# Column cuts of the second MoE product: 512-column products parted, first pairs at 280 and 232, last pairs at 304 and 208

## Chip, cores and metric

The kernel runs on one core of a Trainium2 chip. Times are device microseconds of one execution; the time before is the median of three runs, 930.46 us (929.8 to 931.54). The profile is of one further execution of the same kernel, which took 930.22 us.

## What is computed

Chunked attention over 8 batches, 8 heads, 576 positions, in chunks of 64, then a mixture-of-experts layer with a rational activation, all in float32:

```python
scores = scale * np.matmul(q_c, k_c.transpose(0, 1, 2, 4, 3))
scores = scores - np.max(scores, axis=-1, keepdims=True)
attn = np.exp(scores)
attn = attn / (np.sum(attn, axis=-1, keepdims=True) + 1e-09)
out = np.matmul(attn, v_c)
...
h = x @ w_in                      # 4608 x 512 @ 512 x 2048
h2 = h * h
h3 = h2 * h
P = a[0] + a[1] * h + a[2] * h2 + a[3] * h3
Q = 1.0 + np.abs(b[0]) * np.abs(h) + np.abs(b[1]) * h2
g = P / (Q + 1e-06)
return (g @ w_out).astype(np.float32)   # 4608 x 2048 @ 2048 x 512
```

## The kernel before

The 4608 tokens are cut into 18 groups of 256 (`NB`, index n). Of each group the 2048 hidden columns are cut into four stages of 512 (`NST`, index s). A step g is one pair (n, s). Matmul operands are kept as two parts, a rounded one and the rest (wi_hi and wi_lo, wo_hi and wo_lo, xhi and xlo, ghi and glo), and each product is made of three of them.

FF1 (`ff1`, L329) of a step is 48 products: for each of four blocks of 128 hidden columns, four blocks of 128 rows of x, three combinations. The weights part is stationary (128 columns), x is moving (256 columns, the tokens). It writes the PSUM tile ph.

The rational function of ph is worked out on ScalarE and VectorE (`chain_a` to `chain_glo`) and gives ghi and glo.

FF2 (`ff2`, L393) is the other way round: g is stationary (128 tokens), wo is moving (512 output columns). Parts 0 and 1 are the 16 combinations of ghi with wo_hi and wo_lo, part 2 the 8 of glo with wo_hi. Each of the 24 combinations is run as two products of 256 columns with the same stationary operand, columns 0 to 255 and 256 to 511, so a step has 48. Exceptions are the four products of a group that open or close a PSUM bank: these are single ones of 512 columns. FF2 accumulates all four stages of a group in the tile po, two banks (i = 0 and 1 for the two halves of the tokens). The line that picks the cuts:

```python
for c in ([slice(0, DM)] if start or stop else [slice(0, 256), slice(256, DM)]):
```

with `start` in stage 0 at the first wo_hi product of each bank (k of 0 and 2 of part 0), and `stop` in stage 3 at the last glo product of each bank (k of 3 and 7 of part 2). In the built program each product comes with a load of its stationary operand (LDWEIGHTS), also where two in a row have the same.

Attention of the next group runs between: scores and values (`quarters`, L203: 64 small products of 64 x 64 each; tiles pss and psx), and eight transposes (L282, tile pst).

The program is in an order written by hand (`manual_schedule`). Up to step 11 it is the string `START`, in which a letter stands for an operation and a number for a step or group (F, f: FF1; Z, z, y: the three parts of FF2; S scores; T transposes; A values). From step 12 on the loop at L464 writes it: in each step FF1 of step g, then the attention work of the next group that belongs to the stage, then FF2 of step g - 2 (`LAG`). In TensorE's order one group is:

| stage of g | TensorE runs |
|---|---|
| 0 | FF1, scores, FF2 of the previous group's stage 2 |
| 1 | FF1, FF2 of the previous group's stage 3 (two 512-column products at its end), transposes |
| 2 | FF1, values, FF2 of this group's stage 0 (two 512-column products at its start) |
| 3 | FF1, FF2 of this group's stage 1 |

Of the kernel before, what the change touches and what calls it, by code (L numbers as in the profile page):

```python
# [23 lines left out]
DM = 512  # L24
DFF = 2048
FPS = 4
NST = DFF // (128 * FPS)
# [18 lines left out]
)  # L46
FIRST = 12
PL_TAG = {0: "po", 1: "p1"}

PIECES = [(m, fq, k) for m, fq in ((0, 0), (0, 1), (1, 0), (0, 2), (1, 1), (0, 3), (1, 2), (1, 3)) for k in (0, 1)]  # L50
# [3 lines left out]
def tile_chunked_attention_rational_moe(  # L54
# [32 lines left out]
    def bank_pair(tag, name):  # L87
        return ps.tile([P, 2, 512], F32, tag=tag, name=name)
# [56 lines left out]
    def words(j):  # L145
        low, high = raws[j][:, :, 0], raws[j][:, :, 1]
        return low, high, high.bitcast(F32)

    def w_dest(j):
        return place(j, (wi_hi, wo_hi), (wi_lo, wo_lo))  # L150
# [26 lines left out]
    def w_rest(j):  # L177
        val, hi = words(j)[2], w_dest(j)[0]
        pls[j] = bank_pair(PL_TAG.get(j, "pa"), f"pl{j}")
        n = hi.shape[1] // 2  # L180
# [13 lines left out]
    def groups_of(u):  # L194
        return slice(0, NQ) if u is None else slice(u * NHP, (u + 1) * NHP)

    def quarters(out_cols, tile_out, stat, mov, u):
        for g in range(NQ)[groups_of(u)]:
            for par in range(2):
                for c in range(2):  # L200
                    rows = slice(64 * c, 64 * c + 64)
                    cols = slice(g * 128 + par * 64, g * 128 + par * 64 + 64)
                    nc.tensor.matmul(  # L203
                        tile_out[par * 64:(par + 1) * 64, c, out_cols(g)],
                        stat[rows, cols], mov[rows, cols], start=True, stop=True,
                    )
# [12 lines left out]
    def att_s(n, u=None, tag="pa"):  # L219
        pss = have("s", n, lambda: bank_pair(tag, f"pss{n}"))  # L220
        quarters(lambda g: slice(g * 64, g * 64 + 64), pss, loaded["q", n], loaded["k", n], u)
# [68 lines left out]
    def att_av(n, u=None, tag="pa"):  # L290
        psx = have("x", n, lambda: bank_pair(tag, f"psx{n}"))

        def cols(g):
            v, hp = divmod(g, NHP)
            return slice(hp * 128 + v * 64, hp * 128 + v * 64 + 64)

        quarters(cols, psx, loaded["v", n], att["at", n], u)
# [18 lines left out]
    ch, gbuf, obuf = {}, {}, {}  # L316

    def ff1(n, s, tag, part):
        xhi, xlo = xbuf[n]
        if part == 0:  # L320
            ch[n, s] = [bank_pair(tag, f"ph{n}_{s}").rearrange("p a (b t) -> p (a b) t", t=BT), None, None, None]
        ph = ch[n, s][0]
        for fi in range(2 * part, 2 * part + 2):
            f = slice((FPS * s + fi) * P, (FPS * s + fi + 1) * P)
            mm = []
            for cc in range(NHP):
                mm += [(wi_hi, xhi, cc), (wi_hi, xlo, cc), (wi_lo, xhi, cc)]
            for k, (w, x, cc) in enumerate(mm):
                nc.tensor.matmul(ph[:, fi, :], w[:, cc, f], x[:, cc, :], start=(k == 0), stop=(k == len(mm) - 1))  # L329
# [48 lines left out]
        nc.vector.tensor_mul(gbuf[n, s][1], B, A)  # L378


    def ff2(n, s, tag, part):
        if s == 0 and part == 0:
            obuf[n] = bank_pair(tag, f"po{n}")
        ghi, glo = gbuf[n, s]
        if part < 2:
            mm = [(ghi, w, fi, i) for fi in (2 * part, 2 * part + 1) for i in range(2) for w in (wo_hi, wo_lo)]
        else:
            mm = [(glo, wo_hi, fi, i) for i in range(2) for fi in range(FPS)]
        for k, (g, w, fi, i) in enumerate(mm):
            start = s == 0 and part == 0 and k in (0, 2)  # L390
            stop = s == NST - 1 and part == 2 and k in (3, 7)
            for c in ([slice(0, DM)] if start or stop else [slice(0, 256), slice(256, DM)]):
                nc.tensor.matmul(  # L393
                    obuf[n][:, i, c], g[:, fi, i * 128:(i + 1) * 128], w[:, FPS * s + fi, c], start=start, stop=stop,
                )

    def store(n, last=False):

        rows = out[n * BT:(n + 1) * BT, :].rearrange("(u c t) f -> c u t f", u=UPB, c=2)
        o = p2.tile([P, 2, DM], F32, tag="eo", name=f"o{n}")  # L400
        po = obuf.pop(n)
        if last:
            nc.scalar.copy(o[:, 0, :], po[:, 0, :])
            nc.vector.tensor_copy(o[:, 1, :], po[:, 1, :])
        else:
            nc.scalar.copy(o, po)
        for c in range(2):
            for u in range(UPB):
                nc.sync.dma_start(out=rows[c, u], in_=o[64 * u:64 * u + 64, c, :])

    steps = [(n, s) for s in range(NST) for n in (0, 1)] + [(n, s) for n in range(2, NB) for s in range(NST)]
# [34 lines left out]
    for k, letter in enumerate("Ff"):  # L446
        do[letter] = lambda g, k=k: ff1(*steps[g], ph_tag(g), k)
    for k, letter in enumerate("Zzy"):
        do[letter] = lambda g, k=k: ff2(*steps[g], po_tag(steps[g][0]), k)
# [13 lines left out]
    total = len(steps)  # L463
    for g in range(FIRST, total + LAG):  # L464
        n, s = steps[min(g, total - 1)]
# [59 lines left out]
```

## Time and profile before

| | before |
|---|---|
| median of 3 runs | 930.46 us |
| profiled execution | 930.22 us |
| its span, first to last instruction | 928.4 us |
| TensorE matmul busy | 886.0 us (95%), 9306 products |
| TensorE weight loads busy | 867.7 us (93%), 9306 loads |
| VectorE busy | 746.9 us (80%) |
| ScalarE busy | 593.9 us (64%) |
| DMA | 55.87 MB, mean 60 GB/s |

TensorE's matmuls are pipelined: the profile's duration of one (some 280 ns for 256 columns) overlaps the next, so the pace of a run of products is read from start to start, or from the length of a run divided by its products. In the view of the chain each row has the start of a piece in microseconds after the span's start, its length, the engine, the tile written, the line and the number of instructions; consecutive instructions of one line are merged.

### The profile page before, as it was taken

Reading aid. Unit: us, or ns where it says so; the run is one execution under the profiler, and the core shown is the slowest. Engines: PE = TensorE matmul, PEld = TensorE weight load, DVE = VectorE, ACT = ScalarE, POOL = GpSimd, SP = SyncE. Lnnn points to the kernel's source line nnn. Section 1 sums busy time; section 2 is a strip of 40 time slices with the busy share of each in tenths; the row PEclk is TensorE's granted clock in tenths of the full one; section 3 lists DMA queues with packets and bytes.
Section 4 is the critical chain, followed back from the end, with each engine's and each line's share of the span. In section 5 each row is a group of like instructions: output and inputs, shape, how many; then the busy total and the mean of one; then the engine's idle time right before and its main releaser. Section 6 shows DMA issues by size and latency. Waiting matters only on the chain.

```text
span 928.4 us, 20908 instructions
## 1 busy us (share of the span) xinstructions
PE 886.0 (95%) x9306; PEld 867.7 (93%) x9306; DVE 746.9 (80%) x668; ACT 593.9 (64%) x984; POOL 0.8 (0%) x8
## 2 busy tenths in 40 slices
PE   3589899999999999999999999999999999999997
PEld 2578899999999999999999999999999999999997
DVE  5788888798787878787878787878787888878774
ACT  5999688757474747475757575656565656565452
POOL 0000000000000000000000000000000000000000
PEclk9779899999999999999999999999999999999999
DMA  8443531202020202011110202020202020101011
GB/s 295 165 152 137 181 117 44 55 16 92 1 92 1 86 7 63 30 38 55 24 70 10 83 1 92 2 92 1 92 2 92 2 92 2 47 1 24 1 24 23
DMA packets 20601, 55.87 MB, mean 60 GB/s; under 512 B 2592, under 2 KB 2592, under 8 KB 20512
## 3 DMA queue, kind: packets, MB, share of 16 engines
q1 hardware_dynamic: 20512, 54.54, 18.1%
q8 instruction: 73, 1.20, 0.5%
q14 instruction: 16, 0.13, 0.0%
HBM read 45.09 MB, written 9.44 MB: 59 GB/s over the span
## 4 chain that ended last, share of the span: by engine, by line
PE 82%; ACT 12%; DVE 3%; DMA 2%; issue 1%; SPq 0%; ACTq 0%
PE po L393 39%; PE ph L329 38%; ACT raw L162 3%; PE psx L203 2%; DMA raw<-in_w_in 2%; PE pss L203 2%; ACT raw L158 1%; PE pst L282 1%; ACT e L258 1%; ACT wo_hi L169 1%; ACT A L334 1%; ACT A L349 1%; ACT C L341 1%; ACT B L337 1%; ACT A L353 1%
## 5 line engine op out<-in xcount | busy, mean ns | idle before, releaser
L329 PE MATMUL ph<-xhi,wi_hi 128*128 128x256 f32 x1152 | 326.2, 283 | 8.6 <-DVE C L361 5.2
L329 PE MATMUL ph<-xlo,wi_hi 128*128 128x256 f32 x1152 | 324.2, 281 | 1.6 <-DVE xlo L313 1.6
L329 PE MATMUL ph<-xhi,wi_lo 128*128 128x256 f32 x1152 | 323.6, 281 | 0.0
L334 ACT ACTIVATE A<-ph,ab 128x1024 f32<-128x1024 f32 x72 | 81.3, 1129 | 273.7 <-PE ph L329 272.0
L393 PE MATMUL po<-wo_hi,ghi 128*128 128x256 f32 (+1 forms) x1116 | 230.6, 285 | 3.2 <-DVE ghi L366 3.2
L329 PEld LDWEIGHTS ph<-xhi,wi_hi 128*128 128x128 f32 x1152 | 221.5, 192 | 10.1 <-issue 4.1
L393 PE MATMUL po<-wo_lo,ghi 128*128 128x256 f32 x1152 | 227.5, 279 | 0.0
L329 PEld LDWEIGHTS ph<-xlo,wi_hi 128*128 128x128 f32 x1152 | 219.3, 190 | 2.3 <-DVE xlo L313 2.2
L329 PEld LDWEIGHTS ph<-xhi,wi_lo 128*128 128x128 f32 x1152 | 219.5, 191 | 0.0
L345 DVE SCALAR_TENSOR_TENSOR B<-B,ab,A 128x1024 f32<-128x1024 f32 x72 | 92.4, 1284 | 112.9 <-ACT B L337 112.9
L393 PEld LDWEIGHTS po<-wo_lo,ghi 128*128 128x128 f32 x1152 | 177.9, 188 | 1.6
L393 PEld LDWEIGHTS po<-wo_hi,ghi 128*128 128x128 f32 x1116 | 171.1, 188 | 5.7 <-DVE ghi L366 3.4
L393 PE MATMUL po<-wo_hi,glo 128*128 128x256 f32 (+1 forms) x1116 | 146.9, 284 | 1.9 <-DVE glo L378 1.9
L393 PEld LDWEIGHTS po<-wo_hi,glo 128*128 128x128 f32 x1116 | 137.2, 189 | 3.2 <-DVE glo L378 2.4
L366 DVE SCALAR_TENSOR_TENSOR ghi<-C,ab,A 128x1024 fp32r<-128x1024 f32 x72 | 92.4, 1284 | 11.0 <-ACT A L353 2.4
L349 ACT ACTIVATE A<-B,cst 128x1024 f32<-128x1024 f32 x72 | 83.9, 1166 | 26.4 <-DVE B L345 26.3
L361 DVE SCALAR_TENSOR_TENSOR C<-C,ab,ph 128x1024 f32<-128x1024 f32 x72 | 92.2, 1280 | 3.2 <-ACT B L337 1.0
L374 DVE SCALAR_TENSOR_TENSOR B<-C,ab,B 128x1024 f32<-128x1024 f32 x72 | 92.5, 1285 | 2.4
L378 DVE TENSOR_TENSOR glo<-B,A 128x1024 fp32r<-128x1024 f32 x72 | 88.2, 1225 | 6.8
L357 DVE TENSOR_TENSOR C<-C,ph 128x1024 f32<-128x1024 f32 x72 | 87.5, 1215 | 4.5 <-ACT B L337 3.6
L370 DVE SCALAR_TENSOR_TENSOR B<-B,ghi 128x1024 f32<-128x1024 f32 x72 | 88.2, 1225 | 2.3
L341 ACT ACTIVATE C<-ph,ab 128x1024 f32<-128x1024 f32 x72 | 88.0, 1222 | 2.5 <-DVE B L374 2.3
(53 smaller groups left out, 712.4 us busy)
## 6 DMA issues: line engine op xcount, KB each, us to landing
v<-in_vP SPq DMA_DIRECT2D x18, 512.0 KB, 4.0
out<-o SPq DMA_DIRECT2D x72, 128.0 KB, 2.4
raw<-in_w_in SPq DMA_DIRECT2D x8, 1024.0 KB, 6.6
raw<-in_w_out SPq DMA_DIRECT2D x8, 1024.0 KB, 5.9
qk<-in_qT SPq DMA_DIRECT2D x16, 512.0 KB, 4.7
qk<-in_kT SPq DMA_DIRECT2D x16, 512.0 KB, 5.7
Aqk<-in_qT SPq DMA_DIRECT2D x2, 256.0 KB, 3.4
Bqk<-in_kT SPq DMA_DIRECT2D x2, 256.0 KB, 4.0
```

The costliest lines, as they stand in the source:

```text
L329: nc.tensor.matmul(ph[:, fi, :], w[:, cc, f], x[:, cc, :], start=(k == 0), stop=(k == len(mm) - 1))
L334: nc.scalar.activation(ch[n, s][1], ch[n, s][0], AF.Abs, scale=b0)
L341: nc.scalar.activation(ch[n, s][3], ch[n, s][0], AF.Identity, bias=a2, scale=a3)
L345: nc.vector.scalar_tensor_tensor(B, B, b1a, A, ALU.mult, ALU.add)
L349: nc.scalar.activation(A, B, AF.Ln, bias=cst[:, 0:1], scale=2.0 ** -KLN)
L357: nc.vector.tensor_mul(C, C, h)
L361: nc.vector.scalar_tensor_tensor(C, C, a1, h, ALU.add, ALU.mult)
L366: nc.vector.scalar_tensor_tensor(gbuf[n, s][0], C, a0, A, ALU.add, ALU.mult)
L370: nc.vector.scalar_tensor_tensor(B, B, CQ, gbuf[n, s][0].bitcast(F32), ALU.add, ALU.mult)
L374: nc.vector.scalar_tensor_tensor(B, C, a0, B, ALU.add, ALU.subtract)
L378: nc.vector.tensor_mul(gbuf[n, s][1], B, A)
L393: nc.tensor.matmul(obuf[n][:, i, c], g[:, fi, i * 128:(i + 1) * 128], w[:, FPS * s + fi, c], start=start, stop=stop,)
```

## The change

No product of FF2 has 512 columns any more: each combination is run as two. The cut between the two is column 256, with two exceptions. The first pair of a step's FF2 is cut at 280 (280 and 232 columns) where the matmuls issued last before it were `quarters`, that is scores or values. The last pair of a step's FF2 is cut at 304 (304 and 208 columns), except in the last three steps of the kernel. A small record, `before`, holds which of the three functions issued matmuls last while the program is written. The flag `start` is on the first product of a bank alone, `stop` on the last alone.

```diff
+CUT_FIRST, CUT_LAST = 24, 48
...
+    before = [""]
+
     def quarters(out_cols, tile_out, stat, mov, u):
+        before[0] = "quarters"
...
     def ff1(n, s, tag, part):
         xhi, xlo = xbuf[n]
+        before[0] = "ff1"
...
         for k, (g, w, fi, i) in enumerate(mm):
-            start = s == 0 and part == 0 and k in (0, 2)
-            stop = s == NST - 1 and part == 2 and k in (3, 7)
-            for c in ([slice(0, DM)] if start or stop else [slice(0, 256), slice(256, DM)]):
+            cut = 256
+            if part == 0 and k == 0 and before[0] == "quarters":
+                cut += CUT_FIRST
+            if part == 2 and k == len(mm) - 1 and (n, s) not in steps[-3:]:
+                cut += CUT_LAST
+            for c in (0, 1):
+                start = s == 0 and part == 0 and k in (0, 2) and c == 0
+                stop = s == NST - 1 and part == 2 and k in (3, 7) and c == 1
+                cols = slice(cut, DM) if c else slice(0, cut)
                 nc.tensor.matmul(
-                    obuf[n][:, i, c], g[:, fi, i * 128:(i + 1) * 128], w[:, FPS * s + fi, c], start=start, stop=stop,
+                    obuf[n][:, i, cols], g[:, fi, i * 128:(i + 1) * 128], w[:, FPS * s + fi, cols], start=start, stop=stop,
                 )
+        before[0] = "ff2"
```

TensorE's program, in the loop, behind values (psx7 are the values of group 7, po6 and ghi6_0 the FF2 of group 6, stage 0; the last number of a name is a buffer's). Before:

```order
L203 MATMUL psx7_3994<-at7_3936,v7_3459 64x64 x32
L393 MATMUL po6_4043<-wo_hi_69,ghi6_0_3752 128x512
L393 MATMUL po6_4043<-wo_lo_70,ghi6_0_3752 128x256 x2
L393 MATMUL po6_4043<-wo_hi_69,ghi6_0_3752 128x512
L393 MATMUL po6_4043<-wo_lo_70,ghi6_0_3752 128x256 x2
L393 MATMUL po6_4043<-wo_hi_69,ghi6_0_3752 128x256 x2
```

and now:

```order
L207 MATMUL psx7_4018<-at7_3960,v7_3479 64x64 x32
L405 MATMUL po6_4067<-wo_hi_69,ghi6_0_3774 128x280
L405 MATMUL po6_4067<-wo_hi_69,ghi6_0_3774 128x232
L405 MATMUL po6_4067<-wo_lo_70,ghi6_0_3774 128x256 x2
L405 MATMUL po6_4067<-wo_hi_69,ghi6_0_3774 128x256 x2
L405 MATMUL po6_4067<-wo_lo_70,ghi6_0_3774 128x256 x2
```

The two 512-column products have become pairs, the first of them uneven. Behind scores (FF2 of stage 2) the first pair is uneven in the same way, and no 512-column product stood there.

TensorE's program at the end of FF2 of group 6, stage 3, ahead of the transposes of group 8 (pst8) and FF1 of group 7, stage 2 (ph7_2). Before:

```order
L393 MATMUL po6_4043<-wo_lo_70,ghi6_3_4150 128x256 x2
L393 MATMUL po6_4043<-wo_hi_69,glo6_3_4151 128x256 x6
L393 MATMUL po6_4043<-wo_hi_69,glo6_3_4151 128x512
L393 MATMUL po6_4043<-wo_hi_69,glo6_3_4151 128x256 x6
L393 MATMUL po6_4043<-wo_hi_69,glo6_3_4151 128x512
L282 MATMUL pst8_4495<-ident_71,e8_4303 128x128 x8
L329 MATMUL ph7_2_4506<-xhi7_4033,wi_hi_67 128x256
```

and now:

```order
L405 MATMUL po6_4067<-wo_lo_70,ghi6_3_4176 128x256 x2
L405 MATMUL po6_4067<-wo_hi_69,glo6_3_4177 128x256 x14
L405 MATMUL po6_4067<-wo_hi_69,glo6_3_4177 128x304
L405 MATMUL po6_4067<-wo_hi_69,glo6_3_4177 128x208
L286 MATMUL pst8_4523<-ident_71,e8_4329 128x128 x8
L334 MATMUL ph7_2_4534<-xhi7_4057,wi_hi_67 128x256
```

Here too both 512-column products are gone, and the last pair is uneven. At the ends of the other FF2 runs, where FF1 follows directly, the last two of 16 products with glo have become one of 304 and one of 208 columns; nothing else stands differently there. Over the whole program TensorE has 72 products more, 29 first pairs and 69 last pairs are uneven, and the programs of the other engines are unchanged.

## The prediction

> **What bounds the kernel now.** First the page: busy shares, the granted TensorE clock by slices, and the shares of the chain that ended last.
>
> ```profile
> PE 886.0 (95%) x9306; PEld 867.7 (93%) x9306; DVE 746.9 (80%) x668; ACT 593.9 (64%) x984; POOL 0.8 (0%) x8
> PEclk9779899999999999999999999999999999999999
> PE 82%; ACT 12%; DVE 3%; DMA 2%; issue 1%; SPq 0%; ACTq 0%
> ```
>
> TensorE is busy 95% of the span and holds 82% of the chain, at full clock after the first fifth. A busy share of pipelined matmuls doesn't say how quick they go, so the second view is the chain in order of time over one turn of the loop (start us, us, what): ph is FF1, po FF2, pss scores, psx values, pst transposes.
>
> ```profile
> 430.43 5.44 PE po L393 x48
> 435.87 5.65 PE ph L329 x48
> 441.52 1.09 PE pss L203 x64
> 442.62 5.64 PE po L393 x48
> 448.26 5.66 PE ph L329 x48
> 453.92 5.66 PE po L393 x46
> 459.58 0.87 PE pst L282 x8
> 460.45 5.46 PE ph L329 x48
> 465.91 1.09 PE psx L203 x64
> 467.00 5.85 PE po L393 x46
> 472.85 5.46 PE ph L329 x48
> 478.30 5.44 PE po L393 x48
> 483.75 5.65 PE ph L329 x48
> ```
>
> Each piece begins where the last ended: nothing but TensorE is on the path, and what it saves here the kernel saves. And the same work has **two paces**. 48 products of 256 columns take 5.44 to 5.46 us (113.3 ns each) or 5.65 to 5.66 (117.8). FF2 has it too: 5.44 directly behind a quick FF1, 5.66 behind a slow one; behind scores or values, where some 0.2 us of entry is in the piece, 5.64 or 5.85. A stretch keeps the pace with which it begins. In this turn four of the eight stretches are slow: 435.87, 448.26, 453.92 and 467.00.
>
> The third view, busy times of stretches (span; PE, PEld, DVE, ACT, POOL; clock), says that this isn't the clock, and how often the turn occurs.
>
> ```profile
> 435.71:483.58 47.87, 47.87 (x518) 47.26 (x517) 38.87 (x35) 29.24 (x56) 0.00 (x0) 1.00 0.15 46
> 244.22:866.57 622.35, 622.35 (x6711) 614.47 (x6709) 505.28 (x443) 380.19 (x716) 0.00 (x0) 1.00 0.13 41
> ```
>
> The clock is 1.00 throughout, and 622.35 / 47.87 is 13 turns. VectorE works 38.87 us of the 47.87, so a turn of 47.1 us leaves it 8 us. The chain outside these turns:
>
> ```profile
> 157.63 4.15 ACT e L258 x28
> 169.18 5.92 PE ph L329 x48
> 190.85 5.65 PE po L393 x48
> 196.50 5.45 PE ph L329 x48
> 203.05 5.85 PE po L393 x48
> 208.89 5.66 PE ph L329 x48
> 214.55 5.66 PE po L393 x46
> 227.63 5.85 PE po L393 x46
> 866.73 5.66 PE ph L329 x48
> 872.39 5.66 PE po L393 x48
> 888.97 5.46 PE ph L329 x48
> 894.43 5.64 PE po L393 x46
> 900.07 5.66 PE ph L329 x48
> 905.73 16.98 PE po L393 x142
> ```
>
> Until about 167 us the chain goes through ScalarE and VectorE (the 157.63 row is of that stretch), so a faster TensorE brings nothing there; from 169.18 on it is TensorE's.
>
> What sets a stretch's pace? The rows give four rules. FF2 directly behind FF1 inherits: 472.85 and 478.30 are both quick, 448.26 and 453.92 both slow. FF1 behind a quick FF2 is slow (430.43 then 435.87, 442.62 then 448.26); behind a slow FF2 it is mostly quick (467.00 then 472.85), but not always (894.43 then 900.07). Behind the transposes it is quick (460.45). And a 512-column product ends a quick pace: 894.43 follows the quick FF1 of 888.97 and would inherit 5.44, but begins with such a product and takes 5.64.
>
> **The change part by part.** Only PE's program differs.
>
> *The 72 products of 512 columns go* and become 144 of two parts. What one costs stands in the timeline (start us, us, instruction):
>
> ```profile
> 894.27 0.39 PE L393 MATMUL po<-wo_hi,ghi 128*128 128x512 f32 x1
> 894.49 0.40 PE L393 MATMUL po<-wo_lo,ghi 128*128 128x256 f32 x2
> 894.73 0.40 PE L393 MATMUL po<-wo_hi,ghi 128*128 128x512 f32 x1
> 894.97 0.40 PE L393 MATMUL po<-wo_lo,ghi 128*128 128x256 f32 x2
> ```
>
> The next start comes 0.22 us after the first and 0.24 after the second: as long as two halves at either pace, so parting costs between nothing and 72 x 0.01 = 0.7 us less or more; I take nothing, the 0.22 being 2 x 113 ns to the row's last digit. The added weight load lies under the first half. What it brings is that a quick FF2 stays quick through its start and stop.
>
> *The last pair at 304 and 208.* At 5.44/48 = 113.3 ns per 256 columns, 304 take 134.6 ns and 208 take 92. But the product behind the 208 needs its weights, loaded only once the 208 has begun. The nearest row is the eight transposes, 128 columns and a load each: 0.87/8 = 109 ns; the other end is the 113.3. So the pair takes 243 to 248 ns in place of 226.7: **17 to 21 ns dearer**, I take 19, midway. 69 FF2 runs have it, some 62 of them after 167 us: 62 x 19 ns = **+1.2 us** (1.0 to 1.3). The Trainium skill ("TensorE: Matmul & The Clock Gate", Back-to-back issue gap and LDWEIGHTS) has 2.5 ns + N/2.4 for a product and P/1.2 for a load; by it the pair takes 129.2 + 106.7 in place of 2 x 109.2, 17.5 ns more, and the sum would be +1.1, though it has 109 ns where this trace has 113.3 or 117.8.
>
> *The first pair at 280 and 232* comes 29 times, behind scores or values:
>
> ```profile
> 442.55 0.50 PE L393 MATMUL po<-wo_hi,ghi 128*128 128x256 f32 x2
> 442.88 0.39 PE L393 MATMUL po<-wo_lo,ghi 128*128 128x256 f32 x2
> ```
>
> The second product started 0.50 - 0.28 = 0.22 us after the first: it waits for its weights, and 280 columns (124 ns) are hidden under that. 232 columns (103 ns) are shorter than any load pace above. Cost: nothing (at most 29 x 0.01 = 0.3 if the 280 did show).
>
> *What the two pairs bring* the trace before can't show directly: neither form occurs. Both do one thing: behind the shorter part TensorE waits for the weights with nothing in flight, and the next product begins at another moment against its load. The nearest entry of that kind is that from transposes into FF1 (short products, each waiting for its load), 460.45: quick. Against it speaks the entry behind scores and values, also load-bound, which gave 5.64 at 442.62 and 5.85 at 203.05 and 467.00. So per entry the worth lies between a whole stretch turned quick and one turned slow. I take quick for all, nearest to the 460.45 row, and the rivals hold the other ends.
>
> The sum, each piece at the slow pace replaced by the quick one of the same surroundings: per turn 435.87 5.65 to 5.45 (as 196.50, also ahead of scores), 448.26 5.66 to 5.46, 453.92 5.66 to 5.44, 467.00 5.85 to 5.64: 0.83, times 13 is 10.8. From 190 to 244 us: 190.85, 203.05, 208.89, 214.55, 227.63 give 0.21 + 0.21 + 0.20 + 0.22 + 0.21 = 1.05; from 169 to 190, of 5.92 and some short pieces, 0.4 (0 to 0.7). At the end 0.20 + 0.22 + 0.20 + 0.20, and 16.98 to 144 x 0.1133 = 16.32: together 1.48. Sum 13.7 saved, 1.2 spent. The profiled execution's own time is 930.22 (span 928.4 and 1.8 around it): 917.7; the median shown is 0.24 above it, so **917.9**. Behind a faster TensorE nothing is late: VectorE has the 8 us above. If its cover were gone, TensorE would wait for ghi, and a turn would stay above 38.87.
>
> **The rivals.**
>
> *B: the last pair works, the first doesn't.* For it: FF2 at 203.05 was slow behind scores that followed a quick FF1, and now every FF1 would be quick. Then FF2 behind scores turns slow (-0.21) and FF2 behind values stays so: per turn 0.20 + 0.20 + 0.22 - 0.21 = 0.41, times 13 is 5.3; 0.6 before, 0.4, 1.5 after; less 1.2: **923.9**.
>
> *C: only the price.* The entry doesn't decide, or decides as before, and four of eight stretches stay slow: 930.46 + 1.2 = **931.7**. Against it: 894.43 shows one product's form changing a stretch's pace. The Trainium skill (same page, Step-by-step: what each phase is for) says that weights and moving operand have read ports of their own, so that a load takes nothing from a running matmul. By that one pace is to be had and C follows; the trace, with two paces of one form at clock 1.00, disagrees so far.
>
> *D, on the slower side: the last pair is a bad entry.* If the FF1 behind it begins as FF1 behind a quick FF2 does now, all such FF1 are slow and the FF2 directly behind inherits. Place: 472.85 and 478.30, now quick, 0.20 + 0.22 lost per turn, 5.5 in 13, some 1.2 outside, and the price 1.2: **938.3**. The point where it decides: four last pairs cost 4 x 19 = 76 ns a turn, so the change loses as soon as it doesn't take away at least 0.4 of a slow-paced stretch per turn, net.
>
> **How the numbers follow.** Forecast A 0.47 (its own range 916.3 to 919.6, by the price, the 0 to 0.7 and the parting), B 0.22, C 0.15, D 0.16. A measurement here tells 0.2%, 1.9 us, from no change. A and B are faster: 0.69; C, 931.7, is within 0.2%: 0.15; D is slower: 0.16. The range reaches from A's lower end over B and C, and leaves out D and some 0.04 below: 916.0 to 932.4.
>
> **What would show it.** In the chain of the changed kernel FF1 at 5.44 to 5.48 behind FF2 with its last pair shows the second step right; 5.65 shows it wrong. FF2 behind scores and values at 5.64 shows the first pair right, 5.85 wrong. FF2 behind the last FF1 of a token group at 5.44, start and stop included, shows the 512s to have been what ended the quick pace. The last pair's price stands in the timeline, as the time from the 304 to the first FF1 product. Wrong would be the forecast if pieces of ScalarE or VectorE entered the chain after 250 us, or if entries were not alike from turn to turn.

## The result and the profile after

| | before | changed |
|---|---|---|
| time, median of 4 runs each | 931.0 us (929.8 to 932.11) | 920.46 us (920.09 to 921.43) |
| profiled execution | 930.22 us, span 928.4 | 920.15 us, span 918.3 |

The ratio is 0.9889 [0.9872, 0.9906]: 1.1% faster. The median moved by 10.5 us where 12.6 were forecast.

The page of the changed kernel, busy shares and the chain that ended last:

```profile
PE 874.2 (95%) x9378; PEld 859.6 (94%) x9378; DVE 747.0 (81%) x668; ACT 593.4 (65%) x984; POOL 0.8 (0%) x8
PE 82%; ACT 11%; DVE 2%; DMA 2%; issue 1%; SPq 1%; ACTq 0%
```

TensorE runs 72 products more than before and is busy 11.8 us less (886.0 to 874.2); the busy times of the other engines and the shares of the chain are the same to within 0.5 us and a point. The time has gone out of TensorE's own pace. One turn of the loop, by the chain in order of time (start us, us, what):

```profile
433.46 5.48 PE ph L334 x48
438.94 1.09 PE pss L207 x64
440.03 5.66 PE po L405 x48
445.69 5.48 PE ph L334 x48
451.17 5.45 PE po L405 x48
456.62 0.87 PE pst L286 x8
457.49 5.46 PE ph L334 x48
462.95 1.09 PE psx L207 x64
464.04 5.66 PE po L405 x48
469.70 5.48 PE ph L334 x48
475.19 5.44 PE po L405 x48
480.63 5.48 PE ph L334 x48
```

All eight stretches (a stretch is one FF1 or FF2 of 48 products) have the quick pace, 5.44 to 5.48, or 5.66 with the entry behind scores or values in it. Before, four were slow. The turn is 480.63 - 433.46 = **47.17 us**; it was 483.75 - 435.87 = 47.88.

The start and the end of the part that TensorE bounds, from the same view (the row of 244.76 is cut off where that view ended):

```profile
169.81 5.92 PE ph L334 x48
...
191.56 5.66 PE po L405 x48
197.22 5.66 PE ph L334 x48
202.88 1.09 PE pss L207 x64
203.97 5.85 PE po L405 x48
209.82 5.49 PE ph L334 x48
...
244.76 5.25 PE ph L334 x46
```

```profile
858.02 5.48 PE ph L334 x48
...
896.28 16.34 PE po L405 x144
```

With the rows of before these split the whole gain. The FF1 that opens the first turn starts at 244.76 in place of 244.38: 0.38 us later. Thirteen turns from there (to 858.02, as 866.73 before) take 613.26 in place of 622.35: 9.09 less. From there to the end of the last FF2 it is 912.62 - 858.02 = 54.60 in place of 55.98: 1.38 less. Together 10.1, the difference of the spans.

### The profile page after: what moved, and what is told of

Read it like the earlier page. It is cut to its first block, busy times and chain, and to the rows that moved or that the text cites. A ratio compares the mean times of both kernels' runs of the same rounds, so it can differ in the third digit from the quotient of the medians.

```text
span 918.3 us, 21052 instructions
## 1 busy us (share of the span) xinstructions
PE 874.2 (95%) x9378; PEld 859.6 (94%) x9378; DVE 747.0 (81%) x668; ACT 593.4 (65%) x984; POOL 0.8 (0%) x8
## 4 chain that ended last, share of the span: by engine, by line
PE 82%; ACT 11%; DVE 2%; DMA 2%; issue 1%; SPq 1%; ACTq 0%
PE po L405 39%; PE ph L334 38%; ACT raw L163 3%; PE psx L207 2%; PE pss L207 2%; DMA raw<-in_w_in 2%; ACT raw L159 2%; PE pst L286 1%; ACT e L262 1%; ACT A L339 1%; ACT wo_hi L170 1%; ACT A L354 1%; ACT B L342 1%; ACT C L346 1%; ACT A L358 1%
## 5 line engine op out<-in xcount | busy, mean ns | idle before, releaser
L334 PE MATMUL ph<-xhi,wi_hi 128*128 128x256 f32 x1152 | 325.2, 282 | 10.1 <-DVE C L366 6.7
L405 PE MATMUL po<-wo_hi,ghi 128*128 128x256 f32 (+2 forms) x1152 | 228.9, 280 | 3.2 <-DVE ghi L371 3.2
L405 PEld LDWEIGHTS po<-wo_hi,ghi 128*128 128x128 f32 x1152 | 174.1, 188 | 5.7 <-DVE ghi L371 3.4
L405 PEld LDWEIGHTS po<-wo_lo,ghi 128*128 128x128 f32 x1152 | 174.4, 189 | 0.0
L405 PE MATMUL po<-wo_hi,glo 128*128 128x256 f32 (+2 forms) x1152 | 143.3, 277 | 1.6 <-DVE glo L383 1.6
```

What stands on the lines that cost most here:

```text
L405: nc.tensor.matmul(obuf[n][:, i, cols], g[:, fi, i * 128:(i + 1) * 128], w[:, FPS * s + fi, cols], start=start, stop=stop,)
```

## The experiments

Each kernel ran once, with a run of the kernel before on the same chip beside it. Single times scatter: the chain reaches TensorE's part anywhere from 168.33 to 171.93 us in these runs, ahead of the stretches that are compared here. So the verdicts go by the length of a turn, 47.88 before and 47.17 after, which repeats thirteen times in one run, and by which of its eight stretches are slow. In the view of each kernel's loop the turn repeats to 0.01 us (in p7 below it alternates between two values). The place where one stretch ends and the next begins is called a seam. In the tables the stretches are named by place: A is FF1 ahead of the scores, B FF2 behind them, C and D the next FF1 and FF2, E FF1 behind the transposes, F FF2 behind the values, G and H the next FF1 and FF2. All edits are made to the changed kernel; CUT_FIRST and CUT_LAST are what is added to 256 columns in the first part of the first and of the last pair.

### The parts of the change one by one

```diff
-CUT_FIRST, CUT_LAST = 24, 48
+CUT_FIRST, CUT_LAST = 0, 0     e1_parted_only
+CUT_FIRST, CUT_LAST = 0, 48    e2_last_only
+CUT_FIRST, CUT_LAST = 24, 0    e3_first_only
```

> All pairs cut at 256, no 512-column product. Entry theory (the way a stretch's first product meets its weight load sets the stretch's pace, and the uneven pairs change that): the turn stays at 47.87 us as before, four of eight stretches at 5.65, about 930 us. Rival, the 512-column products alone ended the quick pace: the turn falls to 47.1, about 918 us.

> Only the last pair uneven (304 and 208), first pair at 256. Entry theory: FF1 stays at 5.48 behind FF2, FF2 behind scores and behind values goes from 5.66 to 5.85, the turn from 47.17 to 47.55, about 926 us. Rival, the first pair isn't needed once no product has 512 columns: the turn stays at 47.15.

> Only the first pair uneven (280 and 232), last pair at 256. Entry theory: FF2 behind scores and values stays at 5.66, but each FF1 behind a quick FF2 begins slow and the FF2 directly behind inherits: five stretches slow, the turn about 48.0 us, longer than before, about 934 us. Rival, each uneven pair is worth its own stretches: FF2 behind values gains 0.2 and nothing is lost, the turn 47.65, about 927 us.

| kernel | time us | before, beside it | turn us | slow stretches |
|---|---|---|---|---|
| before | | 930.68 | 47.88 | A, C, D, F |
| e1: 512s parted, all pairs even | 934.66 | 930.68 | 48.28 | B, C, D, F, G, H |
| e2: and the last pair 304 and 208 | 933.42 | 930.68 | 48.14 | B, C, D, E, F |
| e3: and the first pair 280 and 232 | 930.73 | 930.68 | 47.90 | C, D, G, H |
| changed: both | 920.15 | | 47.17 | none |

The turn follows the number of slow stretches, at 0.18 to 0.2 us each. But the parts don't add up. Against the run of before beside them, parting alone costs 4.0 us, parting with the last pair 2.7, parting with the first pair 0.0, and all three together bring 10.1. So neither the expectation nor the rival of e1 and of e2 came out, and e3 came close to the first of its two, with four slow stretches in place of five. The chain of e1 shows why parting alone loses:

```profile
443.45 5.85 PE po L405 x48
449.30 5.66 PE ph L334 x48
454.95 5.66 PE po L405 x48
```

The FF2 behind the scores is slow here (5.85, 5.64 before), as it was in the 203.05 row of the prediction, where a quick FF1 also stood ahead of the scores. The FF1 and FF2 behind it keep its pace; behind the values it goes the same way. With the first pair uneven, e3:

```profile
467.27 5.66 PE po L405 x48
472.93 5.66 PE ph L334 x48
478.59 5.66 PE po L405 x48
```

the FF2 behind scores or values is quick (5.66 has the entry in it; 5.85 in e1). That is what the first pair does. The FF1 behind it is slow and the next FF2 inherits. With only the last pair uneven, e2:

```profile
450.49 5.67 PE ph L334 x48
...
462.68 5.66 PE ph L334 x48
...
475.28 5.48 PE ph L334 x48
```

both FF2 behind scores and values are slow again. Of the two FF1 behind them, each behind a last pair, one is slow (450.49) and one quick (475.28). So the last pair makes FF1 quick behind a quick FF2 (the changed kernel has it at 445.69 and 469.70), but not reliably behind a slow one. And 462.68 is an FF1 behind the transposes that is slow.

### Two products of 512 columns put back

```diff
+            whole = (s == 0 and part == 0 and k == 2) or (s == NST - 1 and part == 2 and k == 3)
+            if whole:
+                cut = DM
-            for c in (0, 1):
+            for c in ((0,) if whole else (0, 1)):
...
-                stop = s == NST - 1 and part == 2 and k in (3, 7) and c == 1
+                stop = s == NST - 1 and part == 2 and k in (3, 7) and (c == 1 or whole)
```

> As the changed kernel, but the second opening product of a group (stage 0) and the first closing one (stage 3) are whole again, 512 columns. If a 512-column product ends a quick pace: FF2 behind values goes from 5.66 to about 5.85 and FF2 of stage 3 from 5.45 to about 5.5, the turn from 47.17 to about 47.4, about 923 us. Rival, the quick pace outlives such a product when the entry was good: the turn stays at 47.17.

934.74 us beside 930.68, turn 48.16, slow stretches A, B, F, G, H. Its chain:

```profile
455.56 5.48 PE po L408 x47
461.03 0.87 PE pst L286 x8
461.90 5.46 PE ph L334 x48
467.36 1.09 PE psx L207 x64
468.45 5.85 PE po L408 x47
474.30 5.66 PE ph L334 x48
479.96 5.66 PE po L408 x48
```

Behind the quick FF1 of 461.90, and with its uneven first pair, the FF2 at 468.45 is slow; it is the one with the 512-column product near its start. The one at 455.56, with a 512 near its end, has lost only some 0.03. The records of single products in its trace show the change of pace itself: their starts are 113 to 115 ns apart up to the 512 and 117 to 119 behind it. So a 512 does end a quick pace, and what follows stays slow for four more stretches, G and A behind uneven last pairs and B behind an uneven first pair among them. The two products cost 48.16 - 47.17 = 0.99 us a turn, four times what was expected. That these 512s go is a condition of the gain, though the parting alone (e1) is a loss.

### Other last pairs

```diff
-CUT_FIRST, CUT_LAST = 24, 48
+CUT_FIRST, CUT_LAST = 24, 32    l1_last32: 288 and 224 columns
+CUT_FIRST, CUT_LAST = 24, 112   l2_last112: 368 and 144
+CUT_FIRST, CUT_LAST = 24, -48   l3_last_m48: 208 and 304
```

> As the changed kernel, last pair at 288 and 224 in place of 304 and 208. Drain theory (it is enough that TensorE waits for weights behind the shorter part; 224 columns, 99 ns, are still shorter than any load pace seen): all stretches stay quick, the turn 47.17 less 4 x 16 columns x 0.44 ns, about 47.14 us. Address theory (the last product should begin at the same place in a 256-byte row of memory as the x that FF1 streams next; at 304 it does, 64 bytes, at 288 it begins at 0): FF1 behind FF2 goes slow, 5.66, and the turn is 47.6 or more.

> As the changed kernel, last pair at 368 and 144. Drain theory and address theory agree that all stretches stay quick (144 columns end early; 368 is 304 + 64 columns, 256 bytes on): the turn is 47.17 plus 4 x 64 columns x 0.44 ns, 47.28 us. If the amount matters otherwise, FF1 behind FF2 goes slow and the turn is 47.6 or more.

> As the changed kernel, but the last pair the other way round, 208 and 304. Drain theory: the longer part now stands last, TensorE has work while FF1's first weights load, FF1 behind a quick FF2 is slow, the turn 47.9 or more. Address theory: the last product begins at 448 + 512 bytes, 192 in its 256-byte row, not x's 64, so slow too. Rival, any uneven last pair will do: the turn stays near 47.17.

| last pair | time us (before beside it: 930.76) | turn us | slow stretches |
|---|---|---|---|
| 288 and 224 | 923.05 | 47.51 | E, F |
| 304 and 208 (the change) | 920.15 | 47.17 | none |
| 368 and 144 | 921.24 | 47.23 | none |
| 208 and 304 | 919.77 | 47.17 | none |

The last row narrows the reason that the prediction gave. The wait for weights that it names is in the traces. In the change the pair itself takes 0.23 us, as two products of 256 do, and the first FF1 product behind the 208 takes 0.13 to the next start in place of 0.113:

```profile
445.30 0.39 PE L405 MATMUL po<-wo_hi,glo 128*128 128x304 f32 x2
445.53 0.30 PE L334 MATMUL ph<-xhi,wi_hi 128*128 128x256 f32 x1
445.66 0.28 PE L334 MATMUL ph<-xlo,wi_hi 128*128 128x256 f32 x1
```

With 208 and 304 the product behind the 208 is the 304 of the same pair, and now it is the pair that takes longer, 0.26 us:

```profile
445.00 0.42 PE L405 MATMUL po<-wo_hi,glo 128*128 128x208 f32 x2
445.26 0.28 PE L334 MATMUL ph<-xhi,wi_hi 128*128 128x256 f32 x1
```

In both, and with 368 and 144, the weight load behind the shorter part's, ahead of an FF1, starts 108 or 109 ns after the one before it, which is the pace of the transposes. So TensorE waits for weights behind the shorter part in either order. With the shorter part first that wait is over before FF1 begins. Yet the chain of that kernel has

```profile
439.73 5.69 PE po L405 x48
445.42 5.45 PE ph L334 x48
450.87 5.46 PE po L405 x48
```

The FF1 behind the pair is quick, at 5.45 even without the 0.03 of the other order; the FF2 that ends with the pair takes 0.01 to 0.03 more instead. So the wait need not stand between the last FF2 product and FF1, as the drain theory of the expectation had it, and the place where the last product begins, the address theory's cause, doesn't decide either. An uneven last pair works in either order. Nor is the wait enough by itself: in e2 and e4 these loads are 108 or 109 ns apart as well, and FF1 behind a slow FF2 stayed slow there (450.49 and 474.30).

How uneven it must be isn't smooth: with 288 and 224 FF1 directly behind FF2 is quick (445.67 and 470.06), but the FF1 behind the transposes turns slow, which neither theory had expected:

```profile
457.45 5.66 PE ph L334 x48
...
464.20 5.86 PE po L405 x48
```

The best of these, 919.77, has the turn of the changed kernel, and one run of it doesn't set it apart; none of them is shown to beat the change.

### Where the operands lie in SBUF

If a pace depends on how each load and each product meet, and not on a wait alone, where the two read in SBUF could matter. In the built program the moving operands of FF1 start 64 bytes above a multiple of 256, those of FF2 128 above it; of the stationary operands it is 128 in FF1 and 64 in FF2 (the weights lie at 128, x and g at 64). A small tile that nothing uses, put ahead of x and g, shifts these, and the work tiles of VectorE and ScalarE with them, and leaves the weights; every instruction stays the same. All five start from e1, the kernel with even pairs only. The tile has 16 columns (64 bytes) in p2, 48 in p4, 32 in p5, 8 in p6 and 24 in p7:

```diff
-CUT_FIRST, CUT_LAST = 24, 48
+CUT_FIRST, CUT_LAST = 0, 0
...
     cst = cp.tile([P, 2], F32, tag="cst", name="cst")
+    cp.tile([P, 16], F32, tag="pad", name="pad")
```

> All pairs at 256, no 512-column product (as e1), and 64 bytes of unused memory a partition ahead of the rotating tiles, so that x, ghi and glo begin at the same place in a 256-byte row as the weight matrices (128 and 128 in place of 64 and 128). Address theory: the pace behind FF2 depends on that offset, FF1 behind a quick FF2 is quick without any uneven pair, and the turn falls from e1's 48.28 to 47.5 or less. Rival, addresses don't matter: 48.28 as in e1.

> All pairs at 256 (as e1), and 192 bytes of unused memory a partition ahead of the rotating tiles: x, ghi and glo begin at 0 of a 256-byte row, the weight matrices at 128. So far 64 bytes apart gave two paces (113.3 and 117.8 ns a product) and the same place gave 120.0 throughout. Address theory, second form (the pace is set by how far apart in the 256-byte row the moving and the stationary operand begin, and the entry only picks between the paces that an offset allows): at 128 apart, the farthest, the same for FF1 and FF2, one pace and it is the quick one, 5.44 everywhere behind FF1 and FF2, the turn about 47.0 us, under 920 us without any uneven pair. Rival, the offset of 0 is the exception and any other behaves as e1: the turn 48.28, 934 us.

> All pairs at 256 (as e1), and 128 bytes ahead of the rotating tiles: x, ghi and glo begin at 192 of a 256-byte row, the weight matrices at 128, again 64 apart but the other way round. Address theory, second form: the two paces 113.3 and 117.8 stay, but FF1 and FF2 change places, so that FF1 behind a quick FF2 begins quick and FF2 behind a quick FF1 begins slow; the turn between 47.5 and 48.3. Rival, only the distance counts and not its sign: the same pattern as e1, FF2 directly behind FF1 inherits, the turn 48.28.

> All pairs at 256 (as e1), 32 bytes ahead of the rotating tiles: x, ghi and glo begin at 96 of a 256-byte row, the weight matrices at 128, 32 apart. If only the 64-byte piece counts in which an operand begins, this acts as 64 apart does: 113.3 or 117.8 ns, the pattern of e1, the turn 48.28. If the distance counts in smaller steps, other paces show, between those of 64 apart and the 120.0 of the same place: the turn between 47.2 and 48.7; under 47.2 would be a version that beats the changed kernel without an uneven pair.

> All pairs at 256 (as e1), 96 bytes ahead of the rotating tiles: x, ghi and glo begin at 160 of a 256-byte row, the weight matrices at 128, 32 apart the other way. If only the 64-byte piece counts, this acts as the same place does: 120.0 ns throughout, the turn 48.68. If the distance counts in smaller steps, the paces are those of 32 apart with FF1 and FF2 changing places, the turn between 47.2 and 48.7.

| kernel | x and g start at (weights at 128) | time us | before, beside it | turn us | FF1, FF2 of 48 products, us |
|---|---|---|---|---|---|
| e1 | 64 | 934.66 | 930.68 | 48.28 | 5.45 or 5.66, 5.66 |
| p2 | 128 | 956.6 | 930.76 | 49.50 | 5.76, 5.76 |
| p4 | 0 | 949.1 | 930.52 | 48.99 | 5.69, 5.69 |
| p5 | 192 | 930.99 | 930.52 | 47.85 | 5.44 or 5.66, 5.66 (or quick, 5.64 with the entry in it) |
| p6 | 96 | 943.11 | 932.02 | 48.63 | 5.67, 5.60 |
| p7 | 160 | 943.76 | 932.02 | 48.57 and 48.62 | 5.60, 5.67 to 5.69 |

The chain of p2:

```profile
445.98 5.76 PE ph L335 x48
...
495.48 5.76 PE ph L335 x48
```

Where both operands start alike there is one pace, 5.76/48 = 120.0 ns, slower than either of before, and the turn is 495.48 - 445.98 = 49.50 (a later expectation gives it as 48.68, which was misread). The same instructions at the same clock (1.00 in the loop of both) differ by 64 bytes of address alone. In p5, 64 bytes apart the other way,

```profile
443.89 5.64 PE po L406 x48
449.53 5.44 PE ph L335 x48
454.97 5.66 PE po L406 x48
460.63 0.87 PE pst L287 x8
461.50 5.66 PE ph L335 x48
...
484.99 5.66 PE ph L335 x48
```

both paces are back and FF1 and FF2 have changed places. Now FF1 directly behind FF2 inherits (449.53 is quick behind the quick 443.89, 484.99 slow behind a slow FF2), and FF2 directly behind a quick FF1 is slow, as FF1 behind a quick FF2 was before. At 128 bytes apart (p4) a stretch has one mean pace again, 5.69/48 = 118.5 ns (its single products start 112 to 124 ns apart in a repeating pattern), which felled the expectation that it would be quick; at 32 apart there are 5.60 and 5.67 to 5.69, FF1 and FF2 swapped between p6 and p7. Of the expectations, both sides failed for p2 and p4; the second form of the address theory came out for p5, and for p6 and p7 the distance counts in steps smaller than 64 bytes. Only the kernels with 64 bytes between the starts have stretches at 113.3 ns.

So the operands' addresses decide which paces there are. That a load's reads and a product's reads collide in SBUF is the likeliest reading, but it is argued, not shown. The tiles of VectorE and ScalarE moved too; against them as the cause speaks p2, whose FF2 products between 250 and 850 us took 120.0 ns in the mean where both engines worked (1667 of them) and where ScalarE alone did (405), as did FF1 products where neither did (84). The weights lay at 128 in every run, so the distance isn't parted from the place of x and g as such; that FF1 and FF2 swap between 64 and 192 and between 96 and 160 speaks for the distance.

## Why the prediction was right, and where it missed

The change gained 10.5 us of the 12.6 that were forecast, with the mechanism that carried the forecast (quick stretches in place of slow ones). The measured 920.46 is above 916.3 to 919.6, the range that forecast A gave for itself.

**What bounds the kernel: right.** TensorE alone; nothing new entered the chain, and a turn has VectorE busy 38.87 us, as before.

**Two paces, and quick everywhere: right.** This is the term that carried the forecast, 0.83 us a turn. Measured is 47.88 - 47.17 = 0.71. The difference is what the quick pieces cost at their entries. FF1 behind a last pair takes 5.48 three times a turn, where 5.45 was put in once and 5.46 twice: 0.07. FF2 behind scores and values takes 5.66 where 5.64 was put in, twice: 0.04. The FF2 ahead of the transposes takes 5.45 for 5.44. Together 0.12, of which the prediction had 0.076, all of it the price of the last pairs. For those the 19 ns were right (0.07 + 0.01 for four); "cost: nothing" for the first pair was 20 ns short. The timeline shows the price of the last pair, one product late (start us, us, instruction):

```profile
433.29 0.30 PE L334 MATMUL ph<-xhi,wi_hi 128*128 128x256 f32 x1
433.43 0.28 PE L334 MATMUL ph<-xlo,wi_hi 128*128 128x256 f32 x1
...
433.90 0.28 PE L334 MATMUL ph<-xhi,wi_lo 128*128 128x256 f32 x1
```

The second FF1 product starts 0.14 after the first, and the first five starts take 433.90 - 433.29 = 0.61 where five at the quick pace take 0.57; from the sixth product on they are 113 ns apart. So "a stretch keeps the pace with which it begins" isn't quite right: this one settles within its first six products. Over 13 turns, 9.09 us came where 10.8 less 13 x 0.076 = 9.8 were forecast: **0.7 us of the miss.**

**The start: mis-sized, 1.7 us.** The terms "190 to 244 us, 1.05" and "169 to 190, 0.4", less some 0.1 for their last pairs, asked for 1.35 us; measured is 0.38 the other way. 0.63 of it lies ahead of that part: the chain reached TensorE at 169.81 in place of 169.18. The kernels without the unused tile spread from 168.33 to 170.48 there, so this isn't shown to be a work of the change. The other 1.1 is the step "I take quick for all": up to 209 us no stretch of 48 products was, though two shorter pieces were (24 products at 177.61 in 2.76, 32 at 180.37 in 3.63). FF2 at 191.56 was slow, the FF1 at 197.22 behind its last pair slow too, where before it was quick (196.50, 5.45), and the FF2 at 203.97 slow despite its first pair. The first quick one is 209.82. The last pair is no switch that always makes the next FF1 quick, as e2's 450.49 shows as well.

**The end: right**, 1.38 us, forecast 1.48 less four last pairs.

**A 512-column product ends a quick pace: right** (e4). But "parting costs between nothing and 0.7 us" was true only with the uneven pairs beside it: alone it costs 48.28 - 47.88 = 0.4 us a turn (e1), through the pace of the stretches behind.

**The reason for the uneven pairs: half shown.** "Behind the shorter part TensorE waits for the weights" is in the traces, in either order of the parts. That this wait is what makes the next stretch quick isn't shown: it may lie inside the pair, ahead of the seam (l3), and with the wait in place FF1 was slow in e2, e4 and at the start. What the runs show is less: an uneven pair at the seam, together with the stretch ahead of it, sets the pace of the next stretch, and which paces there are hangs on the operands' addresses. "I take quick for all" came out in the loop, but no row had shown it; that much of the forecast was luck.

**"Behind the transposes it is quick": not general.** E is slow in e2 (462.68) and in l1 (457.45), with the transposes unchanged.

**The rivals.** B, last pair without the first, was to give 923.9; e2, which is that case, has 933.42. The working took each stretch by itself; in the runs a stretch hangs on the one before it round the whole turn, so one bad entry makes up to four more slow (e4). C, only the price, and D, a bad entry, did not come about. By the rule that stood beside C (the Trainium skill, "TensorE: Matmul & The Clock Gate", Step-by-step: what each phase is for: separate read ports, a load takes nothing from a running matmul) there would be one pace; p2 against e1 disagrees, 120.0 against 113.3 or 117.8 ns for the same instructions, though no run shows the two reads collide.

**Open.** Why these cuts and not 288 and 224; why the start needs until 209 us to fall into the quick pace; what it is in the memory that makes the paces. Other places of x and g than these six, a shift of the weights, a shift by a whole 256 bytes and uneven pairs inside FF1 were not tried.

## What to carry to other kernels

Where TensorE bounds a kernel, divide the length of each repeated stretch by its products before believing a busy share: two paces of one form, at full clock, are time that may be had. Try edits at the seams together as well as one by one: here parting alone cost 4.0 us, with either uneven pair it was 2.7 and 0.0, and with both it brought 10.1. And try where the moving and the stationary operand start in SBUF: a tile that nothing uses moved this kernel between 931 and 957 us.

## What the runs showed of the hardware

- For one form, a float32r product of 256 columns with a load of 128 x 128 each, at clock 1.00, the mean time from start to start in a stretch was 113.3, 116.7, 117.8, 118.1 to 118.5 or 120.0 ns, by where x and g start while the weights start at 128 (all modulo 256 bytes): 64 bytes apart 113.3 or 117.8; 32 apart 116.7 and 118.1 to 118.5; 128 apart 118.5; at the same place 120.0.
- At 64 bytes apart whole stretches of 48 products run at one of two paces. Which one goes by the stretch before and the shape of the products at the seam; it is settled within some six products and often kept for several stretches. A 512-column product inside a quick stretch ended the quick pace there, and two of them in a turn of some 380 others cost 0.99 us.
